# Interleaving a long convolution with an MLP mixer in small pieces, with half of the forward exchanges on GpSimd's DMA queue

## Chip, cores, metric

One core of one Trainium2 chip. The metric is the device time of one execution in microseconds (us), the median over several executions. Only one core works. A run counts as slow when it is over 1.5% above the fastest of its kernel; only fast runs are compared.

## The reference

Two branches read the same input `x = A_q` of 2048 rows by 640 columns (bf16) and are added with a gate per row:

```python
g = sigmoid((x * gate_w).sum(-1, keepdims=True))
# branch a: long convolution along the rows
k_shift = sum over t of k shifted down by 3-t rows * shift_k[:, 3-t]
kv      = k_shift * v
y       = irfft(rfft(kv, 4096) * rfft(ssm_k, 4096))[:2048] + kv * ssm_D
a       = q * y
# branch b: mixer
h  = gelu(layernorm(x) @ w1)                # 640 x 640
x1 = x + shift_groups(h) @ w2               # four column groups shifted by +1, -1, +2, -2 rows
b  = x1 + gelu(layernorm(x1) @ w3) @ w4     # 640 x 1536, 1536 x 640
out = g * a + (1 - g) * b
```

## The kernel before

The convolution is a Fourier transform in two stages, made of matmuls. Row `16p + t` of the input lies in partition `p`, slot `t`. The columns are done in two halves of 320 (`dh`), the frequencies in two halves (`h`). For each (dh, h) there is a *kernel pass* (`h_pass`, transforms the filter) and a *forward pass* (`x_pass`, transforms kv, multiplies, and makes the first stage back); for each dh there is one *inverse pass* (`inv`). Each pass works on 8 pairs. Between the two stages the data change places: what lies in 8 partitions with 16 slots each has to lie in 128 partitions. A DMA from SBUF to SBUF does this, here called an *exchange*:

```python
    def exchange(dst, stage, lo):
        nc.sync.dma_start(out=dst, in_=stage.rearrange("(a r) t d -> a r t d", a=8)[:, lo])
```

One exchange is 128 packets of 640 B, 80 KB. All are issued by SyncE, and all have to be waited for.

```python
    def x_pass(dh, h):
        step1(KV, dh, h, False)                     # 16 matmuls with F1, 8 copies to GR
        for kp in range(T1 // 2):
            ps = pst()
            gx = ring.tile([P, 2, DH], BF16, name="gx", bufs=3)
            for j in range(2):
                exchange(gx[:, j, :], GR, 2 * kp + j)
                nc.tensor.matmul(ps[:, j, 0:DH], lhsT=M3[:, 0, :], rhs=gx[:, j, :], start=True, stop=True)
            xs = ring.tile([P, 2, DH], BF16, name="xs")
            nc.scalar.copy(out=xs[:], in_=ps[:, :, 0:DH])
            pq = ring.tile([P, 2, 2, DH], BF16, name="pq", tag="pv", bufs=3)
            nc.vector.tensor_tensor(out=pq[:], in0=xs[:]..., in1=HH[:, 2 * kp:2 * kp + 2], op=ALU.mult)
            pv = pst()
            for j in range(2):
                nc.tensor.matmul(pv[:, j, 0:DH], lhsT=M3[:, 1, :], rhs=pq[:, j, 0, :], ...)
                nc.tensor.matmul(pv[:, j, 0:DH], lhsT=M3[:, 2, :], rhs=pq[:, j, 1, :], ...)
            nc.scalar.copy(out=VR[:, h, 2 * kp:2 * kp + 2, :], in_=pv[:, :, 0:DH])
    ...
    def inv(dh):
        for tp in range(T1 // 2):                   # per pair: 4 exchanges of 80 KB, 4 matmuls, a product with q
            for j in range(2):
                t1 = 2 * tp + j
                for h in range(2):
                    exchange(vx[:, j, h, :], VR[:, h], t1)
                    nc.tensor.matmul(ps[:, j, 0:DH], lhsT=I1[:, h, t1, :], rhs=vx[:, j, h, :], ...)
            ...
    # the main order: the mixer's chunks stand as blocks between the passes
    h_pass(0, 0); ...; kshift(...); ...
    x_pass(0, 0); h_pass(0, 1); w3_chunk(0); x_pass(0, 1); w4_chunk(0)
    h_pass(1, 0); gq_half(0); inv(0); w3_chunk(1)
    x_pass(1, 0); h_pass(1, 1); w4_chunk(1); w3_chunk(2); x_pass(1, 1)
    gq_half(1); inv(1); ...; w4_chunk(2); ...; w3_chunk(3); ...; w4_chunk(3); ...
```

## Time and profile before

Median 526.69 us (524.35 to 529.03, 2 runs). The profiled execution has a span of 522.9 us.

| stage of the profile before | length, us | what runs |
|---|---|---|
| 0 to 142 | 142 | mixer's first half, angles for F1, k products; VectorE is full |
| 142 to 451 | 309 | convolution passes, mixer chunks between them |
| 451 to 475 | 24 | the last inverse pass |
| 475 to 523 | 48 | two mixer chunks, stores |

First the page of the kernel before. Engines are TensorE matmuls (PE), VectorE (DVE), ScalarE (ACT), GpSimd (POOL), SyncE (SP). Each digit is a fortieth of the span: the busy share in tenths, for PEclk the TensorE clock that the throttle granted.

```profile
span 522.9 us, 4484 instructions
...
PE 317.2 (61%) x1597; PEld 159.9 (31%) x1608; DVE 216.5 (41%) x444; ACT 159.0 (30%) x214; POOL 19.7 (4%) x49
...
PE   0196654992146459446945488355488835559797
...
PEclk9998985896555659755965569556579955558899
```

The table by stage of the kernel before: stretch, its length, then busy time and number of instructions of PE, PEld, DVE, ACT, POOL, then clock, DMA share and GB/s.

```profile
0.00:142.00 142.00, 76.27 (x500) 43.37 (x504) 129.34 (x283) 47.74 (x55) 16.96 (x45) 0.85 0.47 156
142.00:451.00 309.00, 186.22 (x797) 87.22 (x802) 64.10 (x126) 105.07 (x153) 2.76 (x4) 0.65 0.25 59
451.00:475.00 24.00, 13.70 (x37) 3.96 (x38) 10.05 (x17) 0.00 (x0) 0.00 (x0) 0.52 0.48 111
475.00:523.00 48.00, 40.98 (x263) 25.38 (x264) 12.96 (x19) 6.14 (x6) 0.00 (x0) 0.95 0.13 48
```

In the first stretch VectorE is busy 129 of 142 us. In the second nothing is full. What TensorE waits for (its instructions, what ended the wait, us in total, times, longest):

```profile
PE ps L407 <- DVE pq L403: 56.8, 32, 4.2
PE ps L385 <- DMA gx<-GR: 48.4, 46, 5.3
...
PE ps L399 <- DMA gx<-GR: 22.3, 7, 7.6
PE ps L428 <- DMA vx<-R_70: 19.4, 35, 3.3
```

L407 is the first matmul after the product in a forward pass: it waits 56.8 us for VectorE, in every one of the 32 pairs. The timeline of one forward pair before shows why (start, duration, instruction, and in brackets the idle time of its engine and what ended it):

```profile
144.78 0.70 ACT L401 CAST xs<-ps 128x640 bf16<-128x640 f32 x1
...
145.51 0.83 DVE L403 TENSOR_TENSOR pq<-xs,R_71 128x1280 bf16<-128x1280 bf16 x1 [0.45 <-ACT xs L401]
...
146.39 0.43 PE L407 MATMUL ps<-pq,M_140 128*128 128x320 bf16 x1 [1.75 <-DVE pq L403]
...
148.24 0.70 ACT L401 CAST xs<-ps 128x640 bf16<-128x640 f32 x1
148.97 0.82 DVE L403 TENSOR_TENSOR pq<-xs,R_71 128x1280 bf16<-128x1280 bf16 x1 [1.13 <-ACT xs L401]
```

Copy, product and matmuls of one pair follow one another, and the next copy comes 3.46 us after the last (148.24 − 144.78). TensorE's matmuls follow the program's order in this trace, so it stands still meanwhile. The inverse pass before waits for its exchanges. The timeline of SyncE alone shows their issuing (SPq):

```profile
285.60 11.95 SPq L364 DMA_DIRECT2D vx<-R_70  x14
```

14 exchanges are issued over 11.95 us, 0.85 us apart on average; 2.3 us of this SyncE waited for a free buffer. These two products are 2.90 us apart. Over the last inverse pass a pair (four exchanges) takes 2.99 us on average (the products from 454.57 to 475.47, seven steps).

### The profile page before, as it was taken

To read this page: it belongs to the slowest core of one execution; us is meant where nothing else is said; L and a number is where in the kernel's file an instruction comes from. 1 tells how busy PE (TensorE), PEld (TensorE's weight loads), DVE (VectorE), ACT (ScalarE), POOL (GpSimd) and SP (SyncE) were. 2 spreads that over 40 slices of the span, in tenths; PEclk is the share of its full clock that TensorE was granted. 3 is DMA by queue.
4 is the path that set the end of the run, shared out by engine and by line. 5 is a ranking of instruction groups with operands and counts; after the bars stand their busy time and mean duration, and the time that the engine had idled before them with its cause. 6 is when DMAs were issued, how large, how long until landed. Compare 5 with 4: busy or idle time off the path is not lost.

```text
span 522.9 us, 4484 instructions
## 1 busy us (share of the span) xinstructions
PE 317.2 (61%) x1597; PEld 159.9 (31%) x1608; DVE 216.5 (41%) x444; ACT 159.0 (30%) x214; POOL 19.7 (4%) x49
## 2 busy tenths in 40 slices
PE   0196654992146459446945488355488835559797
PEld 0163320670022124123611143122055312115455
DVE  6988999999841020321201140121014041344402
ACT  0534553005033423533052016335301633100030
POOL 5121000000200000000000000000000000000000
PEclk9998985896555659755965569556579955558899
DMA  8970206403610250521125510210520241344001
GB/s 326 373 269 0 89 14 140 137 8 146 200 42 8 61 128 13 145 52 38 43 59 127 116 26 0 66 36 2 136 64 0 64 104 36 76 101 150 25 1 50
DMA packets 47638, 45.34 MB, mean 87 GB/s; under 512 B 2688, under 2 KB 44545, under 8 KB 47232
## 3 DMA queue, kind: packets, MB, share of 16 engines
q1 hardware_dynamic: 47616, 45.06, 31.0%
q8 instruction: 12, 0.20, 0.2%
q14 instruction: 10, 0.08, 0.0%
HBM read 21.46 MB, written 2.62 MB: 46 GB/s over the span
## 4 chain that ended last, share of the span: by engine, by line
PE 35%; DVE 26%; DMA 18%; ACT 9%; issue 6%; SPq 3%; POOL 1%; ACTq 0%
DMA gx<-GR 12%; PE ps L451 11%; PE ps L461 10%; DMA vx<-R_70 5%; DVE pq L403 5%; ACT GR L376 4%; PE ps L407 4%; ACT xs L401 4%; DVE bst L220 4%; PE ps L408 3%; SPq L364 3%; DVE R_72 L358 2%; DVE junk L315 2%; DVE R_72 L359 2%; PE ps L302 2%
## 5 line engine op out<-in xcount | busy, mean ns | idle before, releaser
L403 DVE TENSOR_TENSOR pq<-xs,R_71 128x1280 bf16<-128x1280 bf16 x32 | 26.4, 824 | 97.2 <-ACT xs L401 97.2
L407 PE MATMUL ps<-pq,M_140 128*128 128x320 bf16 x64 | 28.7, 449 | 56.8 <-DVE pq L403 56.8
L453 ACT ACTIVATE R_78<-ps 128x1024 bf16<-128x1024 f32 x24 | 24.6, 1024 | 120.8 <-PE ps L451 120.8
L451 PE MATMUL ps<-XNT,R_76 128*128 128x512 bf16 x232 | 56.1, 399 | 5.6 <-DVE XNT L247 4.7
L385 PE MATMUL ps<-gx,M_140 128*128 128x320 bf16 x64 | 27.9, 436 | 49.4 <-DMA gx<-GR 48.4
L461 PE MATMUL ps<-R_72,R_78 128*128 128x320 bf16 x384 | 57.7, 314 | 0.0
L464 DVE SCALAR_TENSOR_TENSOR QX<-ps,OMG,QX 128x640 bf16<-128x640 f32 x16 | 14.1, 884 | 81.3 <-PE ps L461 81.3
L376 ACT CAST GR<-ps 128x640 bf16<-128x640 f32 x64 | 39.1, 733 | 20.7 <-PE ps L373 20.7
L461 PEld LDWEIGHTS <-R_78 128*128 128x128 bf16 x384 | 39.3, 102 | 18.6 <-issue 1.0
L409 ACT CAST R_70<-ps 128x640 bf16<-128x640 f32 x32 | 22.1, 692 | 72.1 <-PE ps L408 72.1
L399 PE MATMUL ps<-gx,M_140 128*128 128x320 bf16 x64 | 24.2, 468 | 22.4 <-DMA gx<-GR 22.3
L386 ACT ACTIVATE R_71<-ps 128x640 bf16<-128x640 f32 x32 | 22.5, 704 | 49.4 <-PE ps L385 49.4
L428 PE MATMUL ps<-vx,I_75 128*128 128x320 bf16 x64 | 25.3, 440 | 19.9 <-DMA vx<-R_70 19.4
L451 PEld LDWEIGHTS <-R_76 128*128 128x128 bf16 x240 | 24.5, 103 | 36.2 <-issue 10.1
L431 DVE TENSOR_TENSOR KV<-ps,KV 128x640 bf16<-128x640 f32 x16 | 13.2, 825 | 52.5 <-PE ps L428 52.5
L241 PE MATMUL pt<-IDN,xn 128*128 128x128 bf16 x160 | 15.1, 254 | 29.4 <-DVE xn L236 29.2
L408 PE MATMUL ps<-pq,M_140 128*128 128x320 bf16 x64 | 30.2, 472 | 0.0
L408 PEld LDWEIGHTS <-M_140 128*128 128x128 bf16 x64 | 8.1, 127 | 70.8 <-issue 67.1
L220 DVE BATCH_NORM_STATS2 bst<-QX 128x6 f32<-128x320 bf16 x64 | 27.7, 468 | 4.3 <-DMA QX<-in_A_q_dram 4.3
L264 PE MATMUL ps<-XNT,R_76 128*128 128x512 bf16 x97 | 25.3, 417 | 5.9 <-ACT XNT L245 5.6
L401 ACT CAST xs<-ps 128x640 bf16<-128x640 f32 x32 | 22.3, 696 | 19.5 <-PE ps L399 19.5
L385 PEld LDWEIGHTS <-M_140 128*128 128x128 bf16 x64 | 4.2, 110 | 71.1 <-DMA gx<-GR 71.1
(79 smaller groups left out, 348.9 us busy)
## 6 DMA issues: line engine op xcount, KB each, us to landing
gx<-GR SPq DMA_DIRECT2D x128, 80.0 KB
R_71<-R_71 SPq DMA_DIRECT2D x16, 320.0 KB
vx<-R_70 SPq DMA_DIRECT2D x64, 80.0 KB
R_70<-in_A_k_dram SPq DMA_DIRECT2D x3, 1120.0 KB
QX<-in_A_q_dram SPq DMA_DIRECT2D x4, 640.0 KB
R_71<-in_A_ssm_k_dram SPq DMA_DIRECT2D x5, 512.0 KB
KV<-in_A_v_dram SPq DMA_DIRECT2D x4, 640.0 KB
KV<-in_A_q_dram SPq DMA_DIRECT2D x8, 320.0 KB
```

The costliest lines, as they stand in the source:

```text
L220: nc.vector.bn_stats(out=st[:, i, j, :], in_=QX[:, s, j * DH:(j + 1) * DH])
L264: nc.tensor.matmul(ps[:, j, :], lhsT=lhsT, rhs=xt[:, k, :], start=(k == 0), stop=(k == DT - 1))
L376: nc.scalar.copy(out=GR[:, 2 * tp:2 * tp + 2, :], in_=ps[:, :, 0:DH])
L385: nc.tensor.matmul(ps[:, j, 0:DH], lhsT=M3[:, 0, :], rhs=gx[:, j, :], start=True, stop=True)
L401: nc.scalar.copy(out=xs[:], in_=ps[:, :, 0:DH])
L403: nc.vector.tensor_tensor(out=pq[:], in0=xs[:].unsqueeze(2).to_broadcast([P, 2, 2, DH]), in1=HH[:, 2 * kp:2 * kp + 2], op=ALU.mult)
L407: nc.tensor.matmul(pv[:, j, 0:DH], lhsT=M3[:, 1, :], rhs=pq[:, j, 0, :], start=True, stop=False)
L408: nc.tensor.matmul(pv[:, j, 0:DH], lhsT=M3[:, 2, :], rhs=pq[:, j, 1, :], start=False, stop=True)
L428: nc.tensor.matmul(ps[:, j, 0:DH], lhsT=I1[:, h, t1, :], rhs=vx[:, j, h, :], start=(h == 0), stop=(h == 1))
L451: nc.tensor.matmul(ps[:, j, :], lhsT=W3[:, k, (f0 + j) * P:(f0 + j + 1) * P], rhs=xt[:, k, :], start=(k == 0), stop=(k == DT - 1))
L453: nc.scalar.activation(out=GTP[:, (3 * c + f0 // 4) % 5, f0 % 4:f0 % 4 + 2, :], in_=ps[:], func=ACT.Gelu_apprx_tanh)
L461: nc.tensor.matmul(ps[:, j, 0:DH], lhsT=GTP[:, (3 * c + f // 4) % 5, f % 4, i * P:(i + 1) * P], rhs=W4[:, f, j * DH:(j + 1) * DH], start=( ...
```

## The change

The intent is to fill the idle time of the passes with the mixer's matmuls, and to make the passes themselves shorter. The parts, (a) to (f) as the prediction names them:

```diff
 # (a) every pass and the mixer become generators that yield (estimated us, lag) after each piece
+    def mix(a, b, ta, tb, each=None):   # takes pieces of a (conv) and b (mixer) so that both shares grow alike;
+        ...                             # a piece of a comes only when its lag has been filled with other pieces
+    m2 = mlp2(); cv = conv()
+    ...
+    mix(cv, m2, 57.4, 86.0)
+    for s in range(12, 16):             # the last four slabs of w4, adds and stores behind it
+        addy(s)
+        for _ in w4_slab(s): pass
+        store(s)
+        for r in range(3 * s - 36, 3 * s - 33): addy(r); store(r)
 # (b) forward pass pipelined by one pair
+    def x_step2(h, lag):
+        pqs = {}
+        for i in range(T1 // 2 + 1):
+            if i < T1 // 2:
+                gx = gx_load(i); ...    # exchange, M3[0] matmuls, copy xs, product pq of pair i
+                pqs[i] = pq
+            if i >= 1:
+                pq = pqs.pop(i - 1); ...# M3[1], M3[2] matmuls and copy to VR of pair i-1
+            yield (0.84 if i else 0.28), (lag if i == T1 // 2 else 1.0)
 # (c) second queue
+    def gx_load(kp):
+        gx = ring.tile([P, 2, DH], BF16, name="gx", bufs=3)
+        for j in range(2):
+            exchange(gx[:, j, :], GR, 2 * kp + j, nc.gpsimd if j else nc.sync)
 # (d) inverse exchanges merged: 32 of 160 KB instead of 64 of 80 KB
-    VR = R3.rearrange("p (h t d) -> p h t d", h=2, t=T1)
+    VR = R3.rearrange("p (t h d) -> p t h d", h=2, t=T1)
-                    exchange(vx[:, j, h, :], VR[:, h], t1)
+                nc.sync.dma_start(out=vx[:, j], in_=VR.rearrange("(a r) t h d -> a r t (h d)", a=8)[:, t1])
 # (e) head: angles of F1 on GpSimd, second LayerNorm's sums by accumulators, gate sum on ScalarE
-            nc.vector.scalar_tensor_tensor(out=n1[:, j * 256:(j + 1) * 256], in0=wcol, scalar=s16[:, t1:t1 + 1],
-                                           in1=ocol, op0=ALU.mult, op1=ALU.add)
+                for c in range(2):
+                    nc.gpsimd.tensor_scalar(out=n1v[:, j, :, c, :], in0=wv[:, :, c, :], scalar1=s16[:, t1:t1 + 1],
+                                            scalar2=6144.0 - 2048.0 * c, op0=ALU.mult, op1=ALU.add)
 # (f) the gate is applied in the last add instead of to q
+    def addy(s):
+        nc.vector.scalar_tensor_tensor(out=QX[:, s, :], in0=KV[:, s, :], scalar=G32[:, s:s + 1], in1=QX[:, s, :], ...)
 # cut: loads of k in halves, the head's new order, smaller statistics groups
```

## The prediction

> **What bounds it now.** Three stretches (table by stage, span 522.9 us). 0–142 us: VectorE is busy 129 of 142 us; its products for the shifted k (four groups of 0.82 us instructions) alone are 52 us. 142–451 us: the convolution passes run one after another and the mixer chunks stand between them as blocks. There nothing is full: TensorE 186 of 309 us at a granted clock of 0.65, ScalarE 105, VectorE 64, DMA 25%. 451–523 us: the last inverse pass, then two mixer chunks.
>
> The passes are bound by latency. The timeline shows a forward pass repeating every 3.46 us per pair: copy 0.70, product 0.82, matmuls, copy. Kernel passes and inverse passes wait for exchanges: SyncE takes about 0.6–0.75 us to issue each, and the first lands 2.5 us later. In these passes the clock is 0.5–0.6; in mixer blocks it is 0.85–1.0. [...]
>
> **What changes.** (a) After the head, mixer pieces of about 1 us are placed between conv pairs. (b) The forward pass is software-pipelined by one pair. (c) Half of the gx exchanges (64) leave SyncE for GpSimd. (d) The inverse's 64 exchanges become 32 of 160 KB. (e) In the head: angles go to GpSimd, the second LayerNorm's sums come from accumulators, the gate sum goes to ScalarE. (f) Scaling q by the gate moves into the final add (16 more three-operand VectorE instructions of about 0.8 us, replacing 32 of 0.3 and 16 of 0.49).
>
> **Costing.** Head: VectorE loses about 7 us of angles, 5 of gate products and half of 28 us of statistics, of which only the first mixer chunk's share lay before 142 us; but it gains the first mixer chunk's normalisations, and all k products still precede the first forward product. The 32 angle instructions on GpSimd hold VectorE's order for perhaps 8 us. Estimate: first forward product at 138 us instead of 142, with 40 mixer matmuls and the first conv step already done.
>
> Mixed stretch: at full clock a 512-column matmul costs 0.217 us and a 320-column one 0.136 (mixer blocks at clock 1.0). About 200 + 590 of them and 80 transposes make 131 us. ScalarE needs about 1.9 us per pair beside the mixer's activations, so pairs run at 2.0–2.5 us. With exchange latencies and W4 and q loads in the exchange queue: 165 us.
>
> The instruction order shows that the mix runs out of mixer early: the end of the last kernel pass, the last forward pass and the inverse stand alone: 3+5+3+18+3+13, about 46 us. Last mixer slabs, adds and stores: 22 us.
>
> Sum: 138+165+46+22 = 371; I predict **374 us**, range **344 to 410**. Faster by over 2%: **0.96**; within: **0.02**; slower: **0.02**.
>
> **In the profile.** TensorE over 80% busy at a clock above 0.85 in the mixed stretch, first forward product near 138 us; forward period about 2 us; total gx wait of TensorE far below before; a poorly filled tail of about 45 us at clock 0.5–0.7, then a dense last chunk. PE busy falls from 317 to about 270 us.
>
> **What would make it wrong.** GpSimd-issued exchanges slow or starved[...]. If each costs over 2 us, kernel passes stay near 20 us and the total nears 410. In-order queues may make each engine wait at every piece (period over 2.8 us). If the clock stays high in the tail too, 345.

The sum comes to 138 + 165 + 46 + 22 = 371 us and the forecast to 374. The profile before has clocks of 0.50 to 0.56 where convolution passes stand alone (142 to 180 us, 451 to 475 us) and 0.95 to 0.99 in mixer blocks (475 to 523 us, 390 to 420 us). The costs of a matmul are the median distances of two starts in that profile, 0.216 us with 512 columns and 0.136 with 320. The 8 us for the angles on GpSimd are the author's guess: the profile before has no such instruction on GpSimd; 12.3 us were measured after.

## More of the kernel before

The timeline of all engines shows the products of two pairs:

```profile
292.62 0.82 DVE L431 TENSOR_TENSOR KV<-ps,KV 128x640 bf16<-128x640 f32 x1 [5.21 <-PE ps L428]
...
295.52 0.82 DVE L431 TENSOR_TENSOR KV<-ps,KV 128x640 bf16<-128x640 f32 x1 [2.08 <-PE ps L428]
```

## The result, and the profile after

The changed kernel takes **388.14 us** (386.70 and 389.58, 2 runs) against 526.69. The ratio is 0.7369 (95% interval 0.7186 to 0.7553). In a later set of six runs it took 387.86 us, ratio 0.734. Ratios are the mean time of one kernel's fast runs over that of the other's in the same rounds, so they are not quite the ratios of the quoted medians.

The page of the changed kernel:

```profile
span 384.8 us, 4609 instructions
...
PE 265.6 (69%) x1594; PEld 151.4 (39%) x1608; DVE 186.2 (48%) x339; ACT 184.7 (48%) x280; POOL 93.2 (24%) x203
...
PE   0004999675697988987499988577997644624595
...
PEclk9999999979699999999789999999899866865589
```

TensorE does the same work in 52 us less busy time (317.2 to 265.6), as the granted clock is higher: 0.900 on average over the span against 0.728. The same 320-column matmuls of a forward pass (L440 after, L407 before) took 323 ns on average, against 449 before. The mixed stretch was granted 0.96 with TensorE 82% busy, the passes before (142 to 451 us) 0.65 with TensorE 60% busy; what sets the clock no run isolates. The low digits are left at the end, which the table by stage of the changed kernel shows (columns as before):

```profile
0.00:135.00 135.00, 84.99 (x579) 51.65 (x586) 108.64 (x234) 78.72 (x127) 62.03 (x150) 0.95 0.47 139
135.00:302.00 167.00, 136.47 (x813) 78.18 (x821) 48.24 (x70) 86.36 (x124) 25.26 (x44) 0.96 0.45 92
302.00:336.00 34.00, 16.94 (x73) 7.96 (x71) 6.60 (x8) 18.96 (x29) 5.89 (x11) 0.75 0.64 131
336.00:366.00 30.00, 13.01 (x42) 4.22 (x41) 8.84 (x11) 0.69 (x1) 0.00 (x0) 0.54 0.44 104
366.00:385.00 19.00, 14.16 (x92) 9.40 (x90) 13.91 (x18) 0.00 (x0) 0.00 (x0) 0.86 0.32 112
```

The stretch from 135 to 302 us is the mixed one: TensorE 82% busy (136.47 of 167) at a clock of 0.96. From 302 the mixer is used up and the convolution stands alone: 34 us for the end of the last kernel pass and the last forward pass, 30 us for the last inverse pass, then 19 us of mixer, adds and stores. What TensorE waits for in the changed kernel (the first line belongs to the head, where it waits for VectorE's normalised rows):

```profile
PE pt L260 <- DVE xn L257: 39.2, 4, 11.7
PE ps L458 <- DMA vx<-R_70: 24.0, 23, 4.2
PE ps L429 <- DMA gx<-GR: 19.6, 9, 5.7
PE ps L414 <- DMA gx<-GR: 15.3, 15, 2.2
PE ps L440 <- DVE pq L433: 5.2, 7, 1.3
```

The wait for the product fell from 56.8 to 5.2 us and that for gx from 70.7 (48.4 + 22.3) to 34.9. The wait for the inverse exchanges (vx) did not fall: 19.4 to 24.0 us, although there are half as many. The last inverse pass in the timeline after:

```profile
337.34 8.62 SPq L456 DMA_DIRECT2D vx<-R_70  x7
...
340.74 0.71 PE L458 MATMUL ps<-vx,I_75 128*128 128x320 bf16 x2 [4.15 <-DMA vx<-R_70]
342.33 0.69 PE L458 MATMUL ps<-vx,I_75 128*128 128x320 bf16 x2 [0.88 <-DMA vx<-R_70]
...
343.93 0.71 PE L458 MATMUL ps<-vx,I_75 128*128 128x320 bf16 x2 [0.91 <-DMA vx<-R_70]
```

One exchange of 160 KB arrives each 1.6 us, so a pair takes 3.2 us (3.19 on average over the pass, products from 343.06 to 365.40), no less than the 2.99 before. An exchange issued by GpSimd also arrives later than one by SyncE. At the start of the last forward pass both go out at nearly the same time:

```profile
314.98 3.19 SPq L387 DMA_DIRECT2D gx<-GR  x3
315.25 1.75 POOL L387 DMA_DIRECT2D gx<-GR  x3 [11.24 <-ACT GR L400]
...
317.73 0.45 PE L429 MATMUL ps<-gx,M_103 128*128 128x320 bf16 x1 [4.68 <-DMA gx<-GR]
...
319.44 0.42 PE L429 MATMUL ps<-gx,M_103 128*128 128x320 bf16 x1 [1.27 <-DMA gx<-GR]
```

SyncE's is used 2.75 us after its issue, GpSimd's 4.19 us. In the head, VectorE waits for the angles that GpSimd now makes, 12.3 us in four waits:

```profile
10.54 16.41 POOL L170 TENSOR_SCALAR R_78<-HT 128x128 int32<-128x128 f32 x32 [1.97 <-DVE HT L149]
```

### The profile page after: what moved, and what is told of

Same layout as the page of the kernel before. It is cut to its first block, busy times and chain, and to the rows that moved or that the text cites. A ratio compares the mean times of both kernels' runs of the same rounds, so it can differ in the third digit from the quotient of the medians.

```text
span 384.8 us, 4609 instructions
## 1 busy us (share of the span) xinstructions
PE 265.6 (69%) x1594; PEld 151.4 (39%) x1608; DVE 186.2 (48%) x339; ACT 184.7 (48%) x280; POOL 93.2 (24%) x203
## 4 chain that ended last, share of the span: by engine, by line
DMA 23%; issue 20%; DVE 19%; PE 19%; POOL 8%; ACT 6%; SPq 4%; DVEq 0%; ACTq 0%; POOLq 0%
DMA gx<-GR 18%; PE ps L496 5%; PE ps L509 5%; ACT GR L400 4%; POOL R_78 L170 4%; SPq L456 3%; DVE R_72 L372 3%; DMA vx<-R_70 3%; DVE R_72 L375 2%; DVE QX L485 2%; DVE bst L230 2%; DVE QX L318 2%; DMA QX<-in_A_q_dram 2%; PE ps L440 2%; PE ps L315 1%
## 5 line engine op out<-in xcount | busy, mean ns | idle before, releaser
L387 POOL DMA_DIRECT2D gx<-GR x64 | 38.4, 602 | 210.6 <-ACT GR L400 138.3
L496 PE MATMUL ps<-XNT,R_76 128*128 128x512 bf16 x230 | 61.6, 391 | 1.1 <-ACT GR L400 0.3
L509 PE MATMUL ps<-R_72,R_78 128*128 128x320 bf16 x384 | 60.9, 310 | 0.3 <-ACT GR L400 0.2
L509 PEld LDWEIGHTS <-R_78 128*128 128x128 bf16 x384 | 38.8, 101 | 21.9 <-issue 5.2
L260 PE MATMUL pt<-IDN,xn 128*128 128x128 bf16 x160 | 14.1, 242 | 39.3 <-DVE xn L257 39.2
L415 ACT ACTIVATE R_71<-ps 128x640 bf16<-128x640 f32 x32 | 22.3, 700 | 32.0 <-PE ps L414 32.0
L458 PE MATMUL ps<-vx,I_75 128*128 128x320 bf16 x64 | 17.8, 377 | 24.3 <-DMA vx<-R_70 24.0
L496 PEld LDWEIGHTS <-R_76 128*128 128x128 bf16 x240 | 24.0, 101 | 25.0 <-issue 4.4
L429 PE MATMUL ps<-gx,M_103 128*128 128x320 bf16 x64 | 16.2, 332 | 19.8 <-DMA gx<-GR 19.6
L315 PE MATMUL ps<-R_76,R_78 128*128 128x320 bf16 x160 | 27.9, 334 | 2.6 <-issue 2.5
L260 PEld LDWEIGHTS <-xn 128*128 128x128 bf16 x160 | 11.7, 109 | 43.2 <-DVE xn L257 40.5
L257 DVE TENSOR_SCALAR xn<-QX,rs,mb 128x640 bf16<-128x640 bf16 x32 | 13.5, 438 | 28.8 <-PE pt L260 23.4
L414 PE MATMUL ps<-gx,M_103 128*128 128x320 bf16 x64 | 16.4, 318 | 15.6 <-DMA gx<-GR 15.3
L442 ACT CAST R_70<-ps 128x640 bf16<-128x640 f32 x32 | 22.3, 696 | 9.4 <-PE ps L441 7.6
L277 PE MATMUL ps<-XNT,R_76 128*128 128x512 bf16 x96 | 24.2, 396 | 2.3 <-ACT XNT L265 2.1
L440 PE MATMUL ps<-pq,M_103 128*128 128x320 bf16 x64 | 19.9, 323 | 5.4 <-DVE pq L433 5.2
```

What stands on the lines that cost most here:

```text
L260: nc.tensor.transpose(out=pt[:, j, k * P:(k + 1) * P], in_=xn[:, k * P:(k + 1) * P], identity=IDN[:])
L277: nc.tensor.matmul(ps[:, j, :], lhsT=lhsT, rhs=xt[:, k, :], start=(k == 0), stop=(k == DT - 1))
L315: nc.tensor.matmul(ps[:, j, 0:DH], lhsT=gst_ap(k, s), rhs=W2[:, k, j * DH:(j + 1) * DH], start=(k == 0), stop=(k == DT - 1))
L387: eng.dma_start(out=dst, in_=stage.rearrange("(a r) t d -> a r t d", a=8)[:, lo])
L415: nc.scalar.activation(out=HH[:, 2 * kp:2 * kp + 2, 0, :], in_=ps[:, :, 0:DH], func=ACT.Copy, scale=1.0 / S)
L442: nc.scalar.copy(out=VR[:, 2 * i - 2:2 * i, h, :], in_=pv[:, :, 0:DH])
```

## The experiments

Twelve kernels ran, the unedited control included, all correct. They ran in four calls, each on a chip of its own. In every call the kernel before was timed too (its median was 527.1 to 529.2 us). The gains in us below are differences of medians; where the runs are of different calls, the ratios to before are the safer comparison, and they agree.

| run | call | median us | ratio to before (95%) |
|---|---|---|---|
| after_again | 1 | 387.86 | 0.7340 (0.7298 to 0.7382) |
| sp_only | 1 | 374.93 | 0.7119 (0.7084 to 0.7154) |
| no_mix | 1 | 460.90 | 0.8734 (0.8683 to 0.8785) |
| vx_pool | 1 | 390.67 | 0.7414 (0.7372 to 0.7456) |
| vr_ports | 2 | 362.48 | 0.6858 (0.6818 to 0.6899) |
| all_ports | 2 | 358.80 | 0.6802 (0.6758 to 0.6845) |
| tail_fill | 2 | 378.05 | 0.7163 (0.7118 to 0.7208) |
| dve_angles | 2 | 380.87 | 0.7214 (0.7177 to 0.7251) |
| no_pipe | 3 | 438.63 | 0.8314 (0.8271 to 0.8357) |
| ports_pool | 3 | 354.23 | 0.6715 (0.6675 to 0.6756) |
| best | 3 | 343.15 | 0.6500 (0.6462 to 0.6539) |
| best_pool | 4 | 344.01 | 0.6519 (0.6482 to 0.6556) |

### after_again: the control

The changed kernel once more, unedited.

> The changed kernel itself, as the control on this chip for the runs beside it. Every theory: ratio to the kernel before 0.73 to 0.745, about 388 us; last inverse pass alone on the chip again about 30 us, at about 105 GB/s and half of the DMA engines' time.

It took 387.86 us, 383.31 to 389.96 (the slowest of the six counted as slow). The first result is confirmed.

### no_mix: the interleaving undone

```diff
-    mix(cv, m2, 57.4, 86.0)
+    for _ in cv:
+        pass
+    for _ in m2:
+        pass
```

> Whole convolution first, then the mixer as one block; pipelined passes, queues and head kept. Theory A (interleaving earns most of the gain): conv alone about 220 us from 135 us, then about 95 us of mixer and 20 us of end, 455 to 480 us. Rival C (the software pipelining, queues and head earn most of it): below 430 us. TensorE clock in the conv stretch under A: below 0.7.

460.90 us: the interleaving is worth 73 us. The table by stage of no_mix (columns as before) says more:

```profile
135.00:312.00 177.00, 81.74 (x323) 35.18 (x323) 29.12 (x36) 76.92 (x121) 27.46 (x47) 0.66 0.50 101
312.00:360.00 48.00, 26.00 (x105) 11.28 (x104) 14.40 (x20) 10.14 (x16) 3.44 (x6) 0.59 0.40 93
360.00:460.00 100.00, 95.68 (x619) 58.43 (x616) 36.96 (x51) 20.24 (x20) 0.00 (x0) 1.00 0.08 27
```

The convolution alone, with nothing mixed in, still lasts from its first forward product at 135.6 us to its last inverse product at 356.4, which is 221 us. With the mixer mixed in, the same goes from 135.2 to 365.4, which is 230. So most of the 100 us that the mixer takes by itself was hidden behind the convolution's waits. This suggests that the pace of the mixed stretch is set by the convolution's chain of exchanges, copies and products, though TensorE is 82% busy in it. It does not show it alone, because TensorE's clock was 0.66 in the first stretch of no_mix and 0.96 in the mixed one; sp_only below is the better test.

### no_pipe: the pipelining of the forward pass undone

```diff
-        pqs = {}
-        for i in range(T1 // 2 + 1):
-            if i < T1 // 2:
-                gx = gx_load(i)
+        for i in range(1, T1 // 2 + 1):
+            if True:
+                gx = gx_load(i - 1)
 ...
-                pqs[i] = pq
-            if i >= 1:
-                pq = pqs.pop(i - 1)
+            if True:
                 pv = pst()
```

> The changed kernel with the forward pass not pipelined: each piece makes the exchange, the copy, the product and the inverse-side matmuls of one and the same pair, as in the kernel before; interleaving, queues and all else stay. Theory A (the pipelining is needed inside the mix too, because TensorE takes its instructions in order and stands still through the copy of 0.70 and the product of 0.82 us of the same pair): about 1.9 us for each of 24 mixed pairs, less the gaps that are there anyway, and about 1.8 us for each of the 8 pairs that run alone: +30 to +57 us, 418-445 us. Rival B (mixer pieces between the pairs hide it, only the 8 pairs that run alone pay): 398-412 us.

438.63 us, 51 us more than the control: theory A. TensorE's wait for the product is back:

```profile
PE ps L437 <- DVE pq L432: 43.8, 28, 4.4
```

From first to eighth product, the four forward passes last 28.9, 27.9, 26.7 and 24.2 us, against 15.6, 14.3, 14.7 and 14.4 in the changed kernel: 49 us of the 51 (45 against the control's profile). Mixer pieces between the pairs did not hide a wait inside a pair.

### sp_only: all forward exchanges on SyncE again

```diff
-            exchange(gx[:, j, :], GR, 2 * kp + j, nc.gpsimd if j else nc.sync)
+            exchange(gx[:, j, :], GR, 2 * kp + j, nc.sync)
```

> All gx exchanges on SyncE, nothing else changed. My theory A (most exchange time of the forward and kernel passes hides behind mixer pieces, and the GpSimd exchange lands about 1.5 us later than SyncE's): within 1.5% of the control, 382 to 394 us. Rival B (issue time on SyncE limited the passes, and the second queue relieves it): 64 more issues of 0.6 to 0.75 us come back, 405 us or more.

374.93 us: neither theory, the kernel is **13 us faster** without the second queue. TensorE's waits for gx in sp_only:

```profile
PE ps L429 <- DMA gx<-GR: 17.2, 10, 4.8
PE ps L414 <- DMA gx<-GR: 7.2, 17, 1.0
```

The kernel passes gained most (L414: 15.3 to 7.2 us). The first forward product comes at 131.3 us instead of 135.2, as a kernel pass lies before it. The mixed stretch, from there to the mixer's last W3 matmul, is shortened from 167 to 158 us (131.3 to 289.7), with TensorE busy for the same time (136.4 and 136.2 us, so 86% instead of 82%). So TensorE was not the bound there; the chain of the convolution was. The last inverse pass stayed as it was, as it has no gx.

### vx_pool: every second inverse exchange on GpSimd

```diff
-                nc.sync.dma_start(out=vx[:, j], in_=VR...[:, t1])
+                (nc.gpsimd if j else nc.sync).dma_start(out=vx[:, j], in_=VR...[:, t1])
```

> Every second inverse exchange issued through GpSimd too. Theory A (an exchange issued by SyncE is limited by data rate, because only about eight packets are in flight and half of the engines work, and GpSimd's exchanges can reach other engines): the inverse at the end falls from 30 us to 18 to 22 us, total 374 to 382 us. Rival B (issue cost or fixed latency limits it; 16 issues of 0.6 us are not the limit any more): no change, 386 to 390 us.

390.67 us, no gain. This is about the time that rival B named, but not for B's reason: what follows shows a limit of the rate, not of issue cost or fixed latency. The stretch of the last inverse pass in sp_only:

```profile
324.00:354.00 30.00, 12.45 (x39) 3.95 (x39) 8.24 (x10) 0.74 (x2) 0.00 (x0) 0.57 0.45 104
```

and in vx_pool:

```profile
338.00:368.00 30.00, 10.32 (x35) 3.65 (x35) 7.86 (x10) 1.25 (x2) 4.68 (x8) 0.53 0.62 99
```

The DMA engines are busier (0.62 against 0.45) and move no more (99 against 104 GB/s). The trace's packet records say the same: with SyncE alone (sp_only, 330 to 352 us) 7 to 9 packets are in flight for 88% of the time; in vx_pool (342 to 366 us) it is 14 to 16 for 43% of it, and each takes longer: SyncE's packets of 1280 B 114 ns on average against 89, and GpSimd's packets, of 5120 B for the same rows, 676 ns in the median. So neither the issuing queue nor the busy share of the DMA engines was the limit. By the packet records, the exchanges of 80 KB (before) and of 160 KB (changed kernel, control, sp_only, no_mix) moved 98 to 105 GB/s in the median microsecond of the last inverse pass (those with more than 10 packets in flight, which include other transfers, left out).

What remained was the source. The partitions `16a + lo` that one exchange reads lie 16 apart. That this choice of partitions holds the rate down, no run up to here shows. The next run reads from partitions 4 apart, `32*(lo/4) + 4a + lo%4`.

### vr_ports: the sources of the inverse exchanges 4 partitions apart

On top of sp_only. The last forward stage writes its rows in another order, because two of its masks are generated with permuted columns; the exchange reads from there.

```diff
-            nc.vector.tensor_tensor(out=M3[:, m, :], in0=sn[:, m * P:(m + 1) * P], in1=mask, op=ALU.mult)
+            if m == 0: (as before)
+            else:
+                nc.vector.tensor_tensor(out=M3[:, m, :].rearrange("p (rh a rl) -> p a rh rl", rh=4, a=8),
+                                        in0=sn[...].rearrange("p (a rh rl) -> p a rh rl", rh=4, a=8),
+                                        in1=mask.rearrange("p (a rh rl) -> p a rh rl", rh=4, a=8), op=ALU.mult)
 ...
-                nc.sync.dma_start(out=vx[:, j], in_=VR.rearrange("(a r) t h d -> a r t (h d)", a=8)[:, t1])
+                nc.sync.dma_start(out=vx[:, j], in_=VR.rearrange("(rh a rl) t h d -> rh a rl t (h d)",
+                                                                 rh=4, a=8)[t1 // 4, :, t1 % 4])
```

> All forward exchanges on SyncE, and only the inverse exchanges changed: the rows of VR are stored in another order of partitions (the masks of the last forward stage are generated with permuted columns), so that the 8 source partitions of one exchange are 4 apart (32*(r/4) + 4a + r%4) instead of 16 apart. Bytes, packets, instructions and queues are the same. Theory P [...]: a 1280 B packet falls from 82-90 ns to 40-60 ns, the last inverse pass moves about 200 GB/s at half the DMA share for its bytes and shortens from 30 us to 16-20 us; time 359-366 us against 374.9 with all exchanges on SyncE. Rival L (each of the 8 engines in use needs some 85 ns for a 1280 B descriptor whatever its address, or the issue by SyncE at about 1.5 us per exchange is the limit): nothing moves, 372-378 us, packets 80-90 ns.

The theory is that the choice of the source partitions sets the rate; its figures, about twice the measured 105 GB/s and half of the measured packet times, are the author's estimate.

362.48 us against 374.93: the time that theory P named. Same bytes, packets and queue; only the addresses differ. The stretch of the last inverse pass in vr_ports, in its table by stage, is 9 us shorter:

```profile
322.00:343.00 21.00, 12.54 (x40) 4.20 (x40) 8.43 (x11) 0.69 (x1) 0.00 (x0) 0.55 0.50 149
```

What SyncE waits for from 320 to 345 us in vr_ports (the line of the inverse exchanges waiting for TensorE to free a buffer):

```profile
SPq L461 <- PE ps L463: 2.8, 5, 0.7
```

A pair takes 2.08 us instead of 3.27 in sp_only (the products of the pairs: 328.25 to 342.82, seven steps, against 331.14 to 354.04). A pair is 327,680 B, so 100 GB/s became 157. Packets of 1280 B have a median of 62 ns against 96. The time is in the range of theory P, but the packets (expected 40 to 60 ns) and the rate (about 200 GB/s) fall short of it. SyncE's issuing is not what is left: an issue lasts 0.6 us, SyncE waits for buffers, its last exchange is issued by 337.7 us, and the packet records show at least 8 packets in flight at every moment from 325 to 342 us. At the median of 62 ns, 8 packets of 1280 B at a time make 165 GB/s (an estimate from these numbers). So the pass is still bound by the rate of the exchange; why a packet takes 62 ns and not half of 96 is open.

### all_ports: the forward and kernel passes too

On top of vr_ports, the columns of F1 are generated in the permuted order, and the exchange reads GR in the same way. I1, which is made from F1, is put back in order by 8 matmuls with a permutation matrix.

```diff
-        wcol = f32(iot(256, [[128, 2], [0, 2], [2, 64]], 1), 256)
+        for h in range(2):
+            nc.gpsimd.iota(wi[:, h * P:(h + 1) * P], pattern=[[8, 4], [0, 2], [32, 4], [2, 4]], base=1 + 128 * h, ...)
+        wcol = f32(wi, 256)
 ...
-        eng.dma_start(out=dst, in_=stage.rearrange("(a r) t d -> a r t d", a=8)[:, lo])
+        eng.dma_start(out=dst, in_=stage.rearrange("(rh a rl) t d -> rh a rl t d", rh=4, a=8)[lo // 4, :, lo % 4])
```

> As vr_ports, and the columns of F1 are generated in the permuted order too, so that the sources of the 128 forward exchanges also lie 4 partitions apart; I1 is brought back to its order by 8 extra 512-column matmuls and four ScalarE copies (about 4 us of work at the start of the mixed stretch). Theory P: 640 B packets fall from 42 to 20-30 ns, forward exchanges land sooner (2.7 us after the issue by SyncE to about 2.2), TensorE's gx wait falls below 10 us from 17 + 15; time 3 to 8 us below vr_ports less up to 4 us for the reordering: 353-364 us. Rival F (forward passes are bound by ScalarE and the fixed delay of an exchange, not by its rate): equal to vr_ports or up to 4 us above. Rival L: 375-380 us.

358.80 us, 3.7 less, in the expected range; the intervals of the two ratios overlap, so the size of this step is not settled. The trace agrees: 640 B packets in the mixed stretch fell from a median of 45 to 32 ns (expected 20 to 30), the wait of L414's line from 10.3 (vr_ports) to 4.8 us, and each gap between forward passes with a kernel pass in it shrank by about 2 us (40.5 to 38.4 and 31.8 to 29.6), while the first product came 3 us later because of the reordering. The total gx wait of TensorE was 17.8 us and not under 10: the wait at the start of each pass stays.

### ports_pool: the second queue again, with the new addresses

all_ports with `nc.gpsimd if j else nc.sync` restored.

> As all_ports (358.8 us), with every second forward exchange on GpSimd's queue again, as in the changed kernel. Theory D (the GpSimd half costs its longer delay from issue to landing, 4.2 us against 2.7, wherever the exchanges come from): again 8 to 15 us slower than with all on SyncE, 367-374 us, and the landing of gx from GpSimd still about 4 us. Rival C [...]: 353-361 us.

354.23 us: the time that rival C named, and the penalty of 13 us is gone. Rival C is that the second queue costs nothing, or helps, with the new addresses. The list of DMA issues of after_again (size, median us from issue to landing):

```profile
gx<-GR POOLq DMA_DIRECT2D x64, 80.0 KB, 4.1
```

and of ports_pool:

```profile
gx<-GR POOLq DMA_DIRECT2D x64, 80.0 KB, 2.5
```

So the late landing of GpSimd's exchanges was mostly no property of that queue: GpSimd's packets of 4480 B, the greater part of such an exchange, have a median of 186 ns in a stretch of ports_pool (245 to 298 us) against 518 in one of the changed kernel (240 to 300 us). Why the packets of both queues depend on the source partitions is not shown. Whether the second queue now helps is open: 354.23 against 358.80 says so by 1.3% across two calls, best_pool below does not.

### dve_angles: the angles on VectorE again

```diff
-                for c in range(2):
-                    nc.gpsimd.tensor_scalar(out=n1v[:, j, :, c, :], in0=wv[:, :, c, :], scalar1=s16[:, t1:t1 + 1], ...)
+                nc.vector.scalar_tensor_tensor(out=n1[:, j * 256:(j + 1) * 256], in0=wcol, scalar=s16[:, t1:t1 + 1],
+                                               in1=ocol, op0=ALU.mult, op1=ALU.add)
```

> The changed kernel with the angles of F1 generated on VectorE again, in 16 instructions of 0.43 us as before the change. If VectorE's wait for GpSimd at the start (10.7 us of work in the first 28 us of the trace) pushes the whole head, the first forward product comes 5 to 9 us sooner: 379-383 us against 387.9. If the loads of q or the chain through ScalarE hold the head, the time stays within 2 us: 386-390.

380.87 us, 7.0 less than the control. The first forward product starts at 128.1 us instead of 134.2 (control). VectorE is the busiest engine of the head as a whole (108.64 of 135 us), but at the beginning of the head it stood waiting for the angles, and GpSimd needs 16.4 us (32 instructions on 128 columns, 0.51 us each) for what VectorE does in about 7 (16 instructions on 256 columns, 0.42 us each). As the pieces differ in size, the cost per instruction and that per column are not separated.

### tail_fill: the last mixer slabs, adds and stores taken from behind the last inverse pass

```diff
+        for s in range(12, 16):            # at the end of mlp2()
+            yield from w4_slab(s)
 ...
+            if dh == 1:                    # in inv(), after the product
+                for s in (2 * tp, 2 * tp + 1):
+                    addy(s); fin(s)        # fin: store when both parts of a slab are there
 ...
-    mix(cv, m2, 57.4, 86.0)
-    for s in range(12, 16): (adds, slabs, stores)
+    mix(cv, m2, 57.4, 99.2)
```

> The changed kernel with the last four mixer slabs, the adds and the stores placed in the last inverse pass instead of behind it; same arithmetic and exchanges. If the tail is bound by the rate of the exchanges, TensorE has room there (20 of 30 us idle) and the 19-22 us behind the pass mostly disappear: 372-378 us against 387.9 (10 to 16 us less; the last adds and stores remain). If SyncE's queue (stores between exchanges) or the in-order engines delay the exchanges, the gain is under 5 us: 383-390.

378.05 us, 9.8 less than the control, at the edge of the expected range. The last inverse product comes no later (368.5 against 368.2 us), and 6 us follow it instead of 18. But the reason that I expected, TensorE's room inside the last inverse pass (in the changed kernel it is busy 13.01 of the 30 us from 336 to 366), was not used. TensorE's timeline has the last slab's matmuls (L520) and the first inverse matmuls (L458) here:

```profile
317.76 1.25 PE L520 MATMUL ps<-R,R 128*128 128x320 bf16 x8
...
342.44 0.71 PE L458 MATMUL ps<-vx,I 128*128 128x320 bf16 x2 [4.15 <-DMA vx<-R]
```

The mixer ran out before the last forward pass, so the four slabs filled the gap in front of it, and only the adds and stores lie in the inverse pass. The first product of the last forward pass came 4.3 us later than in the control (325.4 against 321.1), but the pass took 11.3 us instead of 16.2; why it was shorter is open.

### best and best_pool: what the experiments point to

best is all_ports + dve_angles + tail_fill.

> All together: exchanges on SyncE, sources 4 partitions apart, angles on VectorE, last mixer slabs inside the last inverse pass. If the gains add where they lie in different stretches: 358.8 less 7 (angles) less 5 to 10 (tail; the inverse pass that would hide the slabs is now some 17 us instead of 30, so that less than the 10 us of tail_fill are left): 341-348 us. If the sooner head is lost to the next wait (weights, loads) or the stores between the exchanges delay the tail: 349-357 us. Outputs as the reference's.

**343.15 us**, 45 us (11.5%) below the changed kernel and 0.65 of the kernel before. The gains add almost fully: 358.8 − 7.0 − 9.8 = 342.0.

> The fastest kernel so far (343.15 us) with every second forward exchange on GpSimd's queue again. If the second queue helps[...] (ports_pool against all_ports: 354.2 against 358.8 us, from two calls): 336-341 us, ratio to before 0.638-0.646. If that difference was one between two calls and not of the kernels[...]: 342-347 us, ratio 0.648-0.658. Outputs as the reference's.

344.01 us. The second queue neither helps nor costs here, so the 1.3% of ports_pool is not confirmed. The simpler kernel, best, is the one to keep.

## Why the prediction was right, and where its sizes were off

The predicted 374 us (344 to 410) and "faster" held; 388.14 is 14 us above.

- **Head.** Predicted first forward product at 138 us, measured 135.2. The wait of VectorE for GpSimd's angles, put at perhaps 8 us, was 12.3 us in the profile; taking it away gained 7.0 (dve_angles). The change lost time here that it need not have.
- **Mixed stretch.** Predicted 165 us, measured 167; TensorE over 80% at a clock above 0.85 was 82% at 0.96; PE busy about 270 us was 265.6. The size was right, its reason only half, and the close agreement was partly luck. I sized it from TensorE's 131 us of work, filled to 80%, with a second queue that costs nothing. Without that queue (sp_only) the stretch takes 158 us with the same work of TensorE, so my 165 was 7 us too long and the queue's cost made up for it. It also shows that the convolution's chain sets the pace and TensorE merely has little to spare: had TensorE been the bound, the stretch could not have become shorter.
- **Pipelining.** Predicted: pairs at 2.0 to 2.5 us. The changed passes take 14 to 16 us for seven steps, 2.0 to 2.2 each. no_pipe shows that this part alone is worth 51 us, and no_mix that the interleaving is worth 73. If the two add, which no run tested, they make 124 of the 139 us.
- **The mis-sized term: the solo tail.** "3+5+3+18+3+13, about 46 us" was 64 us (302 to 366). End of the kernel pass and first step: 13 instead of 8. First exchange 2.8 (3), forward pass about 19 (18), first inverse exchange 3.4 (3). The inverse pass, put at 13, took 25.5 from its first matmul. I had taken the issue time for its limit and so halved it with the number of exchanges. But the exchange was bound by its data rate, 98 to 105 GB/s, with exchanges of 80 KB and of 160 KB alike. The numbers to see it stood in the profile before: 111 GB/s in the last inverse pass, everything included, and two exchanges of 80 KB in about 1.5 us (2.99 / 2). vr_ports shows the cause as far as a run can: another choice of source partitions alone raised the rate to 157 GB/s and took 12.4 us off.
- **The second queue.** I named "GpSimd-issued exchanges slow" as a way to be wrong and counted the queue as neutral in the sum. It cost 13 us (sp_only). What the runs show: with other source partitions the landing fell from 4.1 to 2.5 us (ports_pool). What makes up the rest no run isolates.
- **Last stretch.** Predicted 22 us, measured 19.

The merged exchanges (d) were not undone alone. That they gained nothing follows from the two kernels' rates (2.99 us per pair before, 3.19 after), not from a run of its own. The traces show packet times and rates for source partitions 16 apart and 4 apart (for the inverse exchange 100 and 157 GB/s); why the two differ is not shown.

## What to carry to other kernels

When a transfer is faster neither with fewer and larger pieces (here 3.19 us per pair after, 2.99 before) nor with a second queue (99 GB/s in vx_pool, 104 in sp_only), divide its bytes by its time first, and then try other partitions to read from: here 8 partitions 16 apart gave 100 GB/s and 8 partitions 4 apart 157. The order of rows in SBUF can be changed in the matmul that writes them, if the rest allows it: in vr_ports this needed no further instruction, in all_ports 8 matmuls, four copies and a first product 3 us later. Interleaving two branches hid one behind the waits of the other here (73 us, no_mix), but the branch with the waits set the pace (the mixed stretch fell from 167 to 158 us with the same work of TensorE, sp_only), so its latencies were still worth shortening; and a wait inside one piece had to be pipelined away, as pieces between did not hide it (51 us, no_pipe). Work moved from a busy engine to a slower idle one (16.4 us on GpSimd, about 7 on VectorE) is of use where the busy engine has something else to do at that moment; in this head it had not (7.0 us lost, dve_angles).
